# Values with the values held in TensorE, row sums in four column groups, and one listed order for the opening

## Chip, core and metric

The kernel runs on one NeuronCore of a Trainium2 chip. The metric is the device time of one execution in microseconds. Before the change the median of four runs is 1032.1 us (1031.84 to 1032.41). Smaller is better.

A core has five engines that run at once, each through its own instruction list in order: TensorE (PE, matrix products, with weight loads shown apart as PEld), VectorE (DVE), ScalarE (ACT), GpSimd (POOL) and SyncE (SP, which only issues transfers). They meet at semaphores. TensorE writes its results into eight banks of accumulator memory, and VectorE or ScalarE must copy a result out before the bank can be used again.

## What is computed

Attention of 49,152 query rows (four images of 12,288) over keys that are a pooled and projected image, followed by a gated feed-forward layer:

```python
def _attn_ref(q, kv, w_sr):                      # q (4, 12288, 128), kv (4, 384, 32, 128)
    r = 4
    kv_pool = kv.reshape(B, H // r, r, W // r, r, C).mean(axis=(2, 4))
    kv_flat = kv_pool.reshape(B, -1, C) @ w_sr   # 768 keys for each image
    k = v = kv_flat
    s = (q @ k.transpose(0, 2, 1)) / np.sqrt(C)
    s = s - s.max(-1, keepdims=True)
    a = np.exp(s)
    a /= a.sum(-1, keepdims=True) + 1e-09
    return a @ v

def _moe_ref(x, w_gate, w_val, w_out):           # d_model 128, d_ff 1536
    gate = np.maximum(x @ w_gate, 0.0)
    val = x @ w_val
    return gate * val @ w_out
```

Keys and values are the same 768 x 128 matrix. The feed-forward layer has one property that the change uses: if a row of x is multiplied by a positive number c, gate and val are multiplied by c each, and the output row by c squared.

## The kernel before, in words

**Tiles.** The queries are cut into 96 tiles of 512 rows (T), 24 for each image; four tiles are a group (GRP). The 768 keys are six chunks of 128 (NJC), the 1536 hidden units twelve blocks of 128 (NFB). For a tile k the work is:

- `scores(k, jc)` (line 245): one 512-wide matmul for a chunk of keys, and ScalarE takes the exponential into `aT[k]` (keys by queries, fp16).
- `values(k, jc, half)` (line 252): the exponentials are the weights held in TensorE, the values with one more column of constants stream past, 129 columns, one matmul for each 128 queries and chunk, so 24 in a tile. The extra column gives the row sums. `keep_sums` and `keep_values` (lines 266 and 270) take the reciprocal and multiply, which gives normalised rows `x16`; these are then turned by a DMA transpose (`x_turn`) or, for tiles 0 and 1, on TensorE (`x_turn_pe`, line 287).
- `value_proj(k, fb)` and `gate_proj(k, fb)` (lines 296 and 305): one 512-wide matmul each for a hidden block; ScalarE copies val out, VectorE forms max(gate, 0) x val into `hT`.
- `out_proj(k, fb)` (line 324): twelve matmuls accumulate the output; `out_turn` (line 337) transposes it on VectorE, and POOL multiplies it by the constant 1 / X_SCALE**2 (line 343) before it is stored.

**The loop.** From k = 3 on (LAG) the loop at line 573 goes through twelve steps for each k. In a step it puts out, in this order, one output matmul of tile k - 4, one value matmul of tile k - 3, a score matmul of tile k or values of tile k - 1, and one gate matmul of tile k - 3. The order in the program is the order on every engine (`manual_schedule`, line 412): nothing is rearranged.

**The opening.** Before the loop, lines 415 to 570 handle the first image's keys and tiles 0 to 3 in an order written out by hand. Loads are issued on SP (lines 422 to 429): the key image comes as three pairs of chunks, four pixel lines for each pair; then the first queries. VectorE adds some of the lines and pixels, and TensorE adds up the rest while it transposes them: `turn_add` (line 177) accumulates several transposes into one bank. The result is projected to keys (`project_chunk`, line 198) and turned again to give the values (`turn_values`, line 214). The first four query tiles are cast to fp16 and transposed on TensorE (lines 124 to 139). Tiles 4 and 5 are loaded on SP (`q_load_tile`), cast on POOL and transposed by DMA (`q_cast_turn_tile`, line 114, transposes issued at line 120). The feed-forward weights are loaded on POOL's queue in halves (lines 522 to 525), each half followed by one of those casts; then come the output weights and the rest of group 1's queries (lines 526 to 532). A small copy called `gate` (line 521) holds POOL until the last key lines arrive, so that the weights don't take bandwidth from them.

In the old kernel the opening ends with tiles 0 and 1 finished up to x. The loop's first pass, k = 3, does tile 0's hidden layer together with what is left of the scores and values of tiles 1 to 3 (lines 604 to 615).

Of the kernel before, what the change touches and what calls it, by code (L numbers as in the profile page):

```python
# [16 lines left out]
def kernel(  # L17
# [40 lines left out]
    X_SCALE = 512.0  # L58
    qk_scale = 1.0 / math.sqrt(C)

    assert C == 128 and N % T == 0 and J == 128 * NJC and D_FF == 128 * NFB
    assert NFB == 2 * NJC and NST % GRP == 0 and W // r == 8 and HC == 64

# [9 lines left out]
    q16s, qTs, q32s = {}, {}, {}  # L73
# [25 lines left out]
    def q_load_plain(i0, i1):  # L99
        q32 = work.tile([128, i1 - i0, NS, C], FP32, tag=f"q32_{i0}", bufs=1, name="q32")  # L100
        nc.sync.dma_start(
            q32, q[0, i0 * T : i1 * T, :].rearrange("(p i s) c -> p i s c", i=i1 - i0, s=NS)
        )
        for i in range(i0, i1):
            q32s[i] = q32[:, i - i0]

    def q_load_tile(i):
        q32 = work.tile([128, T], FP32, tag="o_t", bufs=2, name="q32_tile")
        nc.sync.dma_start(
            q32, q[0, i * T : (i + 1) * T, :].rearrange("(t j s) c -> j t (s c)", j=4, s=NS)  # L110
        )
        q32s[i] = q32.rearrange("p (s c) -> p s c", s=NS)

    def q_cast_turn_tile(i):
        g, at = i // GRP, slice(i % GRP * NS, (i % GRP + 1) * NS)
        if g not in q16s:
            q16s[g] = work.tile([128, GRP * NS, C], FP16, tag="q16", bufs=2, name="q16")
            qTs[g] = work.tile([128, GRP * NS, 128], FP16, tag="qT", bufs=3, name="qT")
        nc.gpsimd.tensor_copy(q16s[g][:, at], q32s.pop(i))
        nc.sync.dma_start_transpose(  # L120
            qTs[g][:, at], q16s[g][:, at].rearrange("p s c -> p (s c)")
        )

    def q_cast(i, engine=nc.vector):
        q16 = work.tile([128, NS, C], FP16, tag="q16s", bufs=3, name="q16s")
        if engine is nc.scalar:
            nc.scalar.copy(q16, q32s[i])
        else:
            nc.vector.tensor_copy(q16, q32s[i])
        q16s[0, i] = q16  # L130

    def q_turn_pe(i):
        q16 = q16s.pop((0, i))
        qt_ps = bank([128, NS, 128], FP16)
        for s in range(NS):
            nc.tensor.transpose(qt_ps[:, s, :], q16[:, s, :], ident16)  # L136
        if i == 0:
            qTs[0] = work.tile([128, GRP * NS, 128], FP16, tag="qT", bufs=3, name="qT")
        nc.vector.tensor_copy(qTs[0][:, i * NS : (i + 1) * NS, :], qt_ps)  # L139
# [10 lines left out]
    def kv_load(b, pair, queues=(nc.sync,)):  # L150
        parts = work.tile([128, r, 2, r, C], FP32, tag="kv_in", bufs=3)
# [3 lines left out]
        for dh in range(r):  # L155
            queues[dh % len(queues)].dma_start(  # L156
                parts[:, dh].rearrange("p h dw c -> p (h dw c)"), rows[dh]
            )
        kv_in[b, pair] = parts
# [3 lines left out]
    def pool_pixels(eng, b, pair, h):  # L163
        parts = kv_in[b, pair]
        s2 = work.tile([128, 2, r, C], FP32, tag="kv_s2", bufs=2)
# [11 lines left out]
    def turn_add(chunk, lines, first=False):  # L177

        if first:
# [7 lines left out]
    def turn_end(chunk, lines, engine=nc.vector):  # L187
        turn_add(chunk, lines)
        if chunk % 2 == 0:
            kv_Ts["pair"] = work.tile([128, 2, 128], FP32, tag="kvT", bufs=2, name="kvT")  # L190
        kvT = kv_Ts["pair"][:, chunk % 2]
        if engine is nc.scalar:
            nc.scalar.copy(kvT, kv_Ts[chunk])
        else:
            nc.vector.tensor_copy(kvT, kv_Ts[chunk])
        kv_Ts[chunk] = kvT

    def project_chunk(jc, engine=nc.vector):
        pr = bank([128, 128])
        nc.tensor.matmul(pr, w_sr_f32, kv_Ts.pop(jc), start=True, stop=True)  # L200
        if engine is nc.scalar:
            nc.scalar.mul(kv16[:, 0, jc, 0:C], pr, 1.0 / (r * r))
        else:
            nc.vector.tensor_scalar(kv16[:, 0, jc, 0:C], pr, 1.0 / (r * r), None, op0=ALU.mult)
# [8 lines left out]

    def turn_values(b, pair):
        vt = bank([128, 2, 128], FP16)
        for h in range(2):
            nc.tensor.transpose(vt[:, h], kv16[:, b, 2 * pair + h, 0:C], ident16)
        nc.vector.tensor_copy(kv16[:, b, 2 * pair : 2 * pair + 2, C : 2 * C], vt)
# [26 lines left out]
    def scores(k, jc):  # L245
        if jc == 0:
            aTs[k] = work.tile([128, NJC, T], FP16, tag="aT", bufs=4, name="aT")
# [39 lines left out]
    def x_turn_pe(k):  # L287
        x16 = x16s.pop(k)
        xt_ps = bank([128, NS, 128], FP16)
        for s in range(NS):  # L290
            nc.tensor.transpose(xt_ps[:, s, :], x16[:, s, :], ident16)  # L291
        xT = work.tile([128, NS, 128], FP16, tag="xT", bufs=5, name="xT")
        nc.vector.tensor_copy(xT, xt_ps)
        xTs[k] = xT.rearrange("c s p -> c (s p)")
# [10 lines left out]
    def gate_proj(k, fb):  # L305
        if fb == 0:
# [8 lines left out]
        if fb == NFB - 1:  # L315
            xTs.pop(k)
# [20 lines left out]
    def out_turn(k):  # L337
# [5 lines left out]
        nc.gpsimd.tensor_scalar(  # L343
            o_sb.rearrange("t j s c -> t s j c"),
            o_t.rearrange("t (s j c) -> t s j c", s=NS, j=4),
            1.0 / X_SCALE**2, None, op0=ALU.mult,
        )
# [70 lines left out]
    nc.gpsimd.tensor_copy(ident16, ident)  # L418
    nc.gpsimd.memset(kv16[:, :, :, 2 * C : 2 * C + 16], 1.0 / X_SCALE)

    w_sr_f32 = const.tile([128, C], FP32)
    kv_load(0, 0, (nc.sync, nc.scalar))
    nc.sync.dma_start(w_sr_f32, w_sr)
    for i in range(0, GRP, 2):
        q_load_plain(i, i + 2)
    for pair in range(1, NJC // 2):
        kv_load(0, pair)
    for i in range(GRP, GRP + 2):
        q_load_tile(i)
# [20 lines left out]
    def attend(k, pair):  # L450
        for jc in (2 * pair, 2 * pair + 1):
            for half in range(2):
                values(k, jc, half)

    def line(pair, dh, h=slice(0, 2)):
        return kv_in[0, pair][:, dh, h]

    def add_lines(pair):
        s2 = work.tile([128, 2, r, C], FP32, tag="kv_s2", bufs=2, name="kv_s2")
        nc.vector.tensor_tensor(s2, line(pair, 0), line(pair, 1), op=ALU.add)  # L460
        return s2

    def add_pixels(s2, halves=(slice(0, 2),)):
        s1 = work.tile([128, r, C], FP32, tag="kv_s1", bufs=2, name="kv_s1")
        s1 = s1.rearrange("p (h i) c -> p h i c", h=2)
        for h in halves:
            nc.vector.tensor_tensor(s1[:, h], s2[:, h, 0:2], s2[:, h, 2:4], op=ALU.add)
        return s1

    def scores_of(k, pair):  # L470
        for jc in (2 * pair, 2 * pair + 1):
            scores(k, jc)

    s1 = add_pixels(add_lines(0))
    for h in range(2):
        turn_add(h, line(0, 2, h), first=True)
    for h in range(2):
        turn_add(h, s1[:, h])
    for h in range(2):
        turn_end(h, line(0, 3, h), (nc.vector, nc.scalar)[h])  # L480
    for h in range(2):
        project_chunk(h, (nc.vector, nc.scalar)[h])
    for i in range(2):
        q_cast(i, (nc.vector, nc.scalar)[i])
        q_turn_pe(i)
    scores_of(0, 0)
    scores_of(1, 0)
    for i in range(2, GRP):
        q_cast(i)
    q_turn_pe(2)  # L490
    turn_values(0, 0)
    q_turn_pe(3)
    scores_of(2, 0)
    scores_of(3, 0)

    halves = (slice(0, 1), slice(1, 2))

    def add_third(pair, s2, h):
        nc.vector.tensor_tensor(s2[:, h], s2[:, h], line(pair, 2)[:, h], op=ALU.add)  # L499

    s2 = add_lines(1)
    for h in halves:
        add_third(1, s2, h)
    s1 = add_pixels(s2, halves)
    attend(0, 0)
    for h in range(2):
        turn_add(2 + h, line(1, 3, h), first=True)
    for h in range(2):
        turn_end(2 + h, s1[:, h], nc.scalar)
    for h in range(2):  # L510
        project_chunk(2 + h, nc.scalar)
    s2 = add_lines(2)
    for k in range(GRP - 1):
        scores_of(k, 1)
    add_third(2, s2, halves[0])
    s1 = add_pixels(s2, halves)
    turn_values(0, 1)
    turn_add(5, line(2, 2, 1), first=True)

    gate = const.tile([128, 1], FP32)  # L520
    nc.gpsimd.tensor_copy(gate, line(2, 2)[:, 0, 0, 0:1])
    for own in (slice(0, D_FF // 2), slice(D_FF // 2, D_FF)):
        nc.gpsimd.dma_start(wv16[:, own], moe_w_val[:, own])
        nc.gpsimd.dma_start(wg16[:, own], moe_w_gate[:, own])
        q_cast_turn_tile(GRP + (own.start > 0))
    nc.gpsimd.dma_start(wo16, moe_w_out.rearrange("(fb f) c -> f fb c", f=128))
    rows = q[0, GRP * T : 2 * GRP * T, :].rearrange("(i t j s) c -> j t i s c", i=GRP, t=32, s=NS)
    for j in range(4):
        nc.gpsimd.dma_start(
# [153 lines left out]
```

The softmax here doesn't subtract the row's maximum and nothing guards it: scores larger than these inputs give would overflow.

## Time and profile before

| | us |
|---|---|
| median of four runs | 1032.1 (1031.84 to 1032.41) |
| the profiled execution, its time | 1031.84 |
| its span in the profile | 1030.1 |
| first matmul of the key pooling (line 182) | 8.95 |
| first output matmul of tile 0 (line 333) | 37.60 |
| VectorE busy in the span | 912.9 (89%) |
| ScalarE busy in the span | 908.9 (88%) |

The profile shows one execution, instruction by instruction. Its times count from the start of the span; the time of a run is a little longer than the span, since it also has what lies around it. "Busy" of TensorE counts a matmul from its start to the modelled end of its result, and consecutive matmuls overlap: a 512-wide one takes 379 ns from start to end, but the next starts after about 216. So for a chain of matmuls the distance between starts is the price of one, not its duration. The granted clock is 1.00 in all stretches that are used here.

Three ways of looking at it are used below. A table by stretches gives the busy time of every engine between two moments. The chain that ended last goes back from the last instruction, at each step to what released it. The groups of instructions by line give their number, mean duration and the idle time ahead of them.

### The profile page before, as it was taken

To read this page: it belongs to the slowest core of one execution; us is meant where nothing else is said; L and a number is where in the kernel's file an instruction comes from. 1 tells how busy PE (TensorE), PEld (TensorE's weight loads), DVE (VectorE), ACT (ScalarE), POOL (GpSimd) and SP (SyncE) were. 2 spreads that over 40 slices of the span, in tenths; PEclk is the share of its full clock that TensorE was granted. 3 is DMA by queue.
4 is the path that set the end of the run, shared out by engine and by line. 5 is a ranking of instruction groups with operands and counts; after the bars stand their busy time and mean duration, and the time that the engine had idled before them with its cause. 6 is when DMAs were issued, how large, how long until landed. Compare 5 with 4: busy or idle time off the path is not lost.

```text
span 1030.1 us, 20013 instructions
## 1 busy us (share of the span) xinstructions
PE 1021.8 (99%) x6560; PEld 543.7 (53%) x6560; DVE 912.9 (89%) x1676; ACT 908.9 (88%) x1745; POOL 280.5 (27%) x289
## 2 busy tenths in 40 slices
PE   8999999999999999999999999999999999999998
PEld 5555555555555555555555555555555555555555
DVE  4889898998989898998989898999898898989898
ACT  4988988888898888888888889888888988889887
POOL 1412146521211124642212121664121221111110
PEclk9999999999999999999999999999999999999999
DMA  8936386462542558726345266683653533513222
GB/s 316 121 59 81 93 189 142 77 93 41 86 73 44 78 121 161 169 52 91 55 65 86 34 85 141 143 170 57 86 71 48 73 53 67 87 33 64 34 42 53
DMA packets 328896, 93.60 MB, mean 91 GB/s; under 512 B 308568, under 2 KB 321752, under 8 KB 328792
## 3 DMA queue, kind: packets, MB, share of 16 engines
q1 hardware_dynamic: 313672, 78.24, 39.3%
q0 software_dynamic: 14688, 12.98, 10.8%
q8 instruction: 51, 0.84, 0.3%
q10 hardware_dynamic: 432, 1.11, 0.3%
q14 instruction: 53, 0.43, 0.2%
HBM read 53.94 MB, written 26.35 MB: 78 GB/s over the span
## 4 chain that ended last, share of the span: by engine, by line
PE 98%; DMA 1%; DVE 0%; ACT 0%; issue 0%; SPq 0%; ACTq 0%
PE bank_ps L298 24%; PE bank_ps L309 24%; PE bank_ps L333 23%; PE bank_ps L260 13%; PE bank_ps L249 12%; PE bank_ps L319 1%; DMA parts<-in_kv_dram 1%; PE bank_ps L182 0%; PE bank_ps L208 0%; PE bank_ps L200 0%; DVE kv_s L499 0%; DVE kv_s L460 0%; SPq L156 0%; PE bank_ps L136 0%; PE bank_ps L291 0%
## 5 line engine op out<-in xcount | busy, mean ns | idle before, releaser
L312 DVE SCALAR_TENSOR_TENSOR hT<-bank_ps,val 128x512 f16<-128x512 f32 x1152 | 757.9, 686 | 90.9 <-ACT val L302 70.6
L302 ACT CAST val<-bank_ps 128x512 f16<-128x512 f32 x1152 | 677.5, 589 | 102.5 <-PE bank_ps L298 100.5
L298 PE MATMUL bank_ps<-xT,wv 128*128 128x512 f16 x1152 | 436.6, 379 | 0.1
L309 PE MATMUL bank_ps<-xT,wg 128*128 128x512 f16 x1152 | 436.6, 379 | 0.0
L333 PE MATMUL bank_ps<-hT,wo 128*128 128x512 f16 x1116 | 423.0, 379 | 0.0
L250 ACT ACTIVATE aT<-bank_ps 128x512 f16<-128x512 f32 x576 | 345.8, 604 | 1.5 <-PE bank_ps L249 1.2
L343 POOL TENSOR_SCALAR o_sb<-o_t 128x512 f32<-128x512 f32 x93 | 138.3, 1487 | 693.9 <-DVE rinv L268 658.1
L260 PEld LDWEIGHTS <-aT 128*128 128x128 f16 x2304 | 177.0, 98 | 132.4
L260 PE MATMUL bank_ps<-kv,aT 128*128 128x129 f16 x2304 | 222.8, 220 | 0.0
L249 PE MATMUL bank_ps<-qT,kv 128*128 128x512 f16 x576 | 216.7, 379 | 0.2 <-DVE qT L139 0.2
L298 PEld LDWEIGHTS <-wv 128*128 128x128 f16 x1152 | 112.7, 98 | 132.3
L309 PEld LDWEIGHTS <-wg 128*128 128x128 f16 x1152 | 112.7, 98 | 67.2 <-DVE x L276 0.2
L333 PEld LDWEIGHTS <-wo 128*128 128x128 f16 x1116 | 109.2, 98 | 65.7
L249 PEld LDWEIGHTS <-kv 128*128 128x128 f16 x576 | 56.1, 98 | 67.8 <-issue 0.7
L276 DVE TENSOR_TENSOR x<-bank_ps,rinv 128x256 f16<-128x256 f32 x190 | 80.6, 424 | 6.6
L341 DVE STREAM_TRANSPOSE o_t<-bank_ps 128x512 f32<-128x512 f32 x93 | 65.7, 706 | 0.0
L86 POOL DMA_DIRECT2D q<-in_q_dram x84 | 46.0, 553 | 0.3 <-issue 0.3
L167 POOL TENSOR_TENSOR s<-parts 128x512 f32<-128x512 f32 x36 | 44.8, 1265 | 0.0
L268 DVE RECIPROCAL rinv<-bank_ps 128x2 f32<-128x2 f32 x192 | 28.1, 146 | 1.2 <-PE bank_ps L260 1.2
L169 POOL TENSOR_TENSOR s<-s 128x512 f32<-128x512 f32 x18 | 22.8, 1267 | 1.4
L171 POOL TENSOR_TENSOR c<-s 128x256 f32<-128x256 f32 x18 | 13.1, 725 | 1.4
L319 PEld LDWEIGHTS <-hT 128*128 128x128 f16 x144 | 10.2, 98 | 5.8
(54 smaller groups left out, 96.9 us busy)
## 6 DMA issues: line engine op xcount, KB each, us to landing
parts<-in_kv_dram SPq DMA_DIRECT2D x46, 512.0 KB, 6.8
out_dram<-o_sb SPq DMA_DIRECT2D x353, 64.0 KB, 2.2
q<-in_q_dram POOLq DMA_DIRECT2D x84, 128.0 KB, 4.9
xT<-x SPq DMA_TRANSPOSE x94, 2.5
out_dram<-o_sb SPq DMA_DIRECT2D x80, 16.0 KB, 1.5
placed<-blocks SPq DMA_DIRECT2D x9, 128.0 KB, 1.8
kvT<-placed SPq DMA_DIRECT2D x36, 32.0 KB, 1.9
parts<-in_kv_dram ACTq DMA_DIRECT2D x2, 512.0 KB, 7.2
```

The lines of the kernel that those rows point to most:

```text
L86: nc.gpsimd.dma_start(q16[32 * j : 32 * (j + 1)].rearrange("t (i s) c -> t i s c", i=GRP), rows[j])
L249: nc.tensor.matmul(s_ps, kv16[:, k // NST, jc, 0:C], qT_of(k), start=True, stop=True)
L250: nc.scalar.activation(aTs[k][:, jc, :], s_ps, AF.Exp, scale=qk_scale)
L260: nc.tensor.matmul(x_ps[:, i, :], aTs[k][:, jc, s * 128 : (s + 1) * 128], kv16[:, k // NST, jc, C : 2 * C + 1], start=(jc == 0 and i == 0) ...
L276: nc.vector.tensor_tensor(x16s[k][:, 2 * half : 2 * half + 2, :], x_ps[:, :, 0:C], rinv.to_broadcast([128, 2, C]), op=ALU.mult,)
L298: nc.tensor.matmul(va_ps, wv16[:, fb * 128 : (fb + 1) * 128], xTs[k], start=True, stop=True)
L302: nc.scalar.copy(val, va_ps)
L309: nc.tensor.matmul(g_ps, wg16[:, fb * 128 : (fb + 1) * 128], xTs[k], start=True, stop=True)
L312: nc.vector.scalar_tensor_tensor(hTs[k][:, fb, :], g_ps, 0.0, vals.pop((k, fb)), op0=ALU.max, op1=ALU.mult)
L333: nc.tensor.matmul(o_banks[k], wo16[:, fb, :], hTs[k][:, fb, :], start=fb == 0, stop=fb == NFB - 1)
L341: nc.vector.transpose(o_t, o_banks.pop(k))
L343: nc.gpsimd.tensor_scalar(o_sb.rearrange("t j s c -> t s j c"), o_t.rearrange("t (s j c) -> t s j c", s=NS, j=4), 1.0 / X_SCALE**2, None, ...
```

## The change

It touches only tiles 0 to 3 and the order of the opening. Beyond that, the loop is the same.

1. **Values.** For tiles 0 to 3 the values are held in TensorE and the exponentials stream past, 512 wide: six matmuls for each tile (`lead_values`) in place of 24, and the result comes out turned already, without normalisation. One copy (`lead_kept`) makes it the input of the feed-forward layer.
2. **Row sums.** Since the extra column is gone, the sums come from matmuls with a 128 x 32 block of ones as weights (`lead_sums`), one for each tile and chunk, 24 in all. Tile k uses the 32 columns of the array from 32k on and writes 32 partitions of one shared bank. They come in two pieces: U0 (five chunks, 20 matmuls) and U1 (the last chunk, four).
3. **Scale at the end.** VectorE turns the sums, takes the reciprocal and squares it; POOL spreads it in 16 small copies (`lead_scales`, R in the list). In `out_turn` POOL multiplies the output of these tiles by that scale, broadcast over 32 columns, in place of the constant.
4. **One list.** The whole opening is one list of words. T0.1 is the transposing of line 1 of chunk 0, T2.p that of pixel sums; a, b, c and p are sums on VectorE; kvT, pj, key, vt and val are the steps to keys and values of a chunk; cast, qt and qT those of the queries; S, V, v and g are scores, values, value and gate projection of a tile; W0 and W1 the weight halves, wo the output weights with the rest of the queries. Keys and values now go chunk by chunk. Tile 0's whole hidden layer and three score matmuls of tile 4 (S4.5, S4.0, S4.2) are in the list; the loop starts at k = 4 and leaves out the scores done. Pooling uses other sums: chunks 0, 1 and 3 entirely by transposes on TensorE, chunk 4 partly, chunks 2 and 5 on VectorE.
5. **Loads.** Queries 2 and 3 are loaded ahead of 0 and 1. W1 is issued before the cast of tile 4, and wo with the remaining queries before the cast of tile 5.

```diff
+    LEAD = GRP
+    OPENING = """
+        T0.1 T1.0 T0.0 T0.2 cast2 T1.2 T1.1 T0.3 cast0 kvT0 qt2 T1.3 cast3 cast1 gate22 W0 W1
+        cast4 qT4 wo cast5 qT5 qt3 pj0 qt0 qT2 kvT1 pj1 key0 qT3 key1 qt1 qT1 S2.0 S3.1 qT0 vt1
+        T3.0 vt0 a2 val1 S3.0 val0 T3.1 S1.1 S2.1 b2 V3.1 S0.1 V3.0 c2 T3.2 S1.0 V2.0 T3.3 kvT3
+        p2 S0.0 V1.0 pj3 V2.1 T2.p key3 V1.1 kvT2 vt3 val3 S3.3 pj2 key2 a4 S2.3 V0.0 V0.1 S0.3
+        S0.2 S1.3 p4 a5 V2.3 S3.2 V3.3 b5 T4.2 V0.3 c5 T4.p T4.3 vt2 kvT4 val2 S2.2 S1.2 p5 pj4
+        V3.2 key4 T5.p kvT5 S0.4 V0.2 S3.4 vt4 pj5 val4 V1.3 key5 S1.4 V0.4 vt5 val5 S0.5 S2.4
+        V3.4 S3.5 S2.5 S1.5 V0.5 U0 xT0 v0.5 V3.5 v0.3 xT3 U1 R v0.1 V1.4 v0.2 g0.5 g0.2 v0.0
+        V2.2 S4.5 g0.3 v0.4 V2.4 v0.11 g0.4 v0.7 g0.1 g0.11 v0.8 v0.9 V1.2 v0.6 g0.7 V2.5 g0.0
+        V1.5 xT1 v0.10 g0.9 xT2 g0.10 S4.0 g0.6 S4.2 g0.8
+    """.split()
...
+    def lead_values(k, jc):
+        first = k not in x_banks
+        if first:
+            x_banks[k], x_count[k] = bank([128, T]), 0
+        x_count[k] += 1
+        nc.tensor.matmul(
+            x_banks[k], kv16[:, 0, jc, C : 2 * C], aTs[k][:, jc, :],
+            start=first, stop=x_count[k] == NJC,
+        )
+
+    def lead_kept(name, k):
+        xTs[k] = work.tile([128, NS, 128], FP16, tag="xT", bufs=5, name="xT").rearrange("c s p -> c (s p)")
+        copy_on(name, xTs[k], x_banks.pop(k))
+
+    def lead_sums(chunks):
+        if "sums" not in x_banks:
+            x_banks["sums"] = bank([128, T])
+        for jc in chunks:
+            for k in range(LEAD):
+                nc.tensor.matmul(
+                    x_banks["sums"][32 * k : 32 * (k + 1), :], ones, aTs[k][:, jc, :],
+                    start=jc == 0, stop=jc == NJC - 1, skip_group_check=True,
+                    tile_position=(0, 32 * k),
+                )
+
+    def lead_scales():
+        turned = work.tile([128, NS * 4, 32], FP32, tag="o_sb", bufs=3, name="sums_turned")
+        nc.vector.transpose(turned.rearrange("p x m -> p (x m)"), x_banks.pop("sums"))
+        inverse = const.tile([128, NS * 4], FP32)
+        nc.vector.reciprocal(inverse, turned[:, :, 0])
+        square = const.tile([128, NS * 4], FP32)
+        nc.vector.tensor_tensor(square, inverse, inverse, op=ALU.mult)
+        for k in range(LEAD):
+            for b in range(4):
+                nc.gpsimd.tensor_copy(
+                    lead_scale[32 * b : 32 * (b + 1), k], square[32 * k : 32 * (k + 1)]
+                )
...
+        if k < LEAD:
+            scale = lead_scale[:, k].rearrange("t (s j o) -> t s j o", s=NS, o=1)
+            nc.gpsimd.tensor_tensor(to, o_by, scale.to_broadcast([128, NS, 4, 32]), op=ALU.mult)
+        else:
+            nc.gpsimd.tensor_scalar(to, o_by, 1.0 / X_SCALE**2, None, op0=ALU.mult)
...
-    for k in range(LAG, last + 1):
+    for word in OPENING:
+        open_step(word)
+    nc.gpsimd.tensor_copy(gate, hTs[0][:, NFB - 1, 0:1])
+    q_load(2)
...
+    for k in range(LEAD, last + 1):
...
-            elif step % 2 == 0:
-                if k < NT:
+            if step % 2 == 0:
+                if k < NT and (k, step // 2) not in done:
                     scores(k, step // 2)
```

Each engine takes its instructions from the list in the list's order. Copies and sums go to VectorE unless a table gives them to ScalarE (kvT0, kvT1, kvT2, kvT5, key2, val3, cast3, qT0, qT2, xT1, xT2) or POOL (the casts of tiles 1, 2, 4 and 5). `aT` has five buffers now instead of four.

## The prediction

> **What bounds the kernel now.** I read three things in this order: the busy times, the busy time by stretch, and the chain that ended last.
>
> ```profile
> PE 1021.8 (99%) x6560; PEld 543.7 (53%) x6560; DVE 912.9 (89%) x1676; ACT 908.9 (88%) x1745; POOL 280.5 (27%) x289
> ```
>
> TensorE bounds everything, so only two things can move the time: how much TensorE work there is, and how long TensorE waits. The stretches (columns: stretch, length, busy us and instructions of PE, weight loads, DVE, ACT, POOL, then clock, DMA share, GB/s) show where it waits.
>
> ```profile
> 8.95:13.00 4.05, 3.64 (x28) 2.98 (x28) 0.98 (x4) 1.04 (x3) 0.00 (x0) 1.00 1.02 409
> 13.00:16.00 3.00, 2.75 (x21) 1.47 (x22) 2.62 (x8) 2.18 (x6) 0.00 (x0) 1.00 1.03 410
> 16.00:20.29 4.29, 3.56 (x27) 2.40 (x25) 3.77 (x6) 2.66 (x7) 0.00 (x0) 1.00 1.02 409
> 20.29:24.00 3.71, 3.71 (x27) 2.73 (x28) 2.29 (x6) 3.36 (x8) 1.40 (x3) 1.00 0.78 203
> 24.00:28.00 4.00, 4.00 (x52) 3.14 (x50) 1.12 (x5) 3.37 (x8) 1.61 (x3) 1.00 0.63 119
> 37.60:46.68 9.08, 9.08 (x44) 4.09 (x43) 8.64 (x16) 9.08 (x19) 2.36 (x5) 1.00 0.63 102
> ```
>
> After 20.29 us TensorE has no hole worth a tenth. What can be won lies before that, in the opening; the start of tile 0's output projection (L333, first matmul at 37.60 in the timeline) is the mark against which I measure. The chain names what fills the holes:
>
> ```profile
> 1.49 7.42 DMA parts<-in_kv_dram
> 8.95 2.40 PE bank_ps L182 x20
> ...
> 15.71 1.23 DVE kv_s L460
> 16.93 0.02 issue
> 16.95 1.29 DVE kv_s L499 x2
> 18.25 0.35 DVE kv_s L467
> 18.59 0.04 issue
> 18.64 0.78 PE bank_ps L182 x4
> ```
>
> Until 8.95 it is the first key rows arriving, and from 15.71 to 18.59 it is VectorE, summing pooled lines while TensorE has nothing to do.
>
> **Price list, from starts in the timeline and chain.** A 512-wide fp16 matmul: 42 of them fill 37.60 to 46.68, so 0.216. A 129-wide one: 16 in 0.91 in the chain, 0.057. A 128-wide fp16 transpose: two in 0.11, 0.056. An fp32 transpose of one pixel: four start between 9.87 and 10.31, 0.110. A key projection: two chunks in 0.83, 0.41. Loads lie under the matmuls:
>
> ```profile
> L298 PE MATMUL bank_ps<-xT,wv 128*128 128x512 f16 x1152 | 436.6, 379 | 0.1
> L298 PEld LDWEIGHTS <-wv 128*128 128x128 f16 x1152 | 112.7, 98 | 132.3
> L260 PE MATMUL bank_ps<-kv,aT 128*128 128x129 f16 x2304 | 222.8, 220 | 0.0
> ```
>
> **Before, 8.95 to 37.60 (28.65 us).** Work: 48 fp32 transposes 5.28, 6 projections 2.46, 16 q, 6 value and 8 x transposes 1.68, 24 scores and 24 hidden-layer matmuls 48 x 0.216 = 10.37, 96 value matmuls 5.47. Sum 25.26, so 3.4 us of holes.
>
> **After, part by part.** *Pooling on TensorE.* The listed order has 16 transposes each for chunks 0, 1 and 3, 10 for chunk 4, 2 each for chunks 2 and 5: 62 in place of 48, 1.5 us more. But T0.1, T1.0 and T0.0 (12 of them, 1.3) need only lines 0 and 1, on which VectorE's first sum already started at 6.38; they fall into the hole before 8.95. Leaves 50, 5.50. The VectorE sums of the first pair (1.23 and 0.69) vanish; those of the second pair shrink to 3 sums of 0.69 and one of 0.42 for chunk 2.
> *Values.* 96 x 0.057 = 5.47 become 24 x 0.216 = 5.18; the 8 x transposes (0.45) go, and so do the normalising reciprocals and multiplications of tiles 0 to 3 on VectorE and ScalarE.
> *Row sums (U).* 24 new matmuls of 32 columns. No row shows matmuls in separate column groups. From below: 24 starts at the shortest spacing any row has, 0.056, 1.34 in all. From above: one after another with the load uncovered, 24 x (0.216 + 0.098) = 7.5; with loads covered, as in the L298 rows, 5.18. A gain is excluded: the old sums rode along as column 129. I take 1.34: the four groups of a chunk write disjoint partitions.
> A rule that speaks against it: the Trainium skill, "TensorEngine Tiling (Array Packing)", Key Properties, says that changing the tiling mode drains TensorE, and "TensorE: Matmul & The Clock Gate", Part 3, gives 2.38x for three column tiles and lets a weight load pass under a running matmul only if its row group differs. The L298 rows disagree with the last point, 98 ns loads lying under matmuls in the same rows with 0.1 us idle over 1152. By those pages I estimate 1.7 (1.34 x 3 / 2.38) plus four drains of 0.16, 2.3 in all, which moves the forecast below by nothing.
> *Moved.* Tile 0's whole first layer and three score matmuls of tile 4 (S4.5, S4.0, S4.2) stand before the loop. So 27 scores, 24 hidden, 24 values: 75 x 0.216 = 16.20; 22 small transposes 1.23; projections 2.46. Sum with U: 5.50 + 2.46 + 1.23 + 16.20 + 1.34 = 26.73, of which 0.65 is later saved in the loop (39 matmuls in place of 42): 26.1 net, 0.8 more than before.
> *Holes left.* Laying the listed order out with these durations, each engine in its own order, leaves 0.9 before S4.5: 0.45 for the first q casts (pair 2-3 usable at 10.34 plus POOL's 0.61 cast), 0.1 before the first scores, the rest eight small waits on VectorE and ScalarE copies. The same laying-out of the old order gives 37.4 for the measured 37.60.
>
> **The new wait.** S4.5 needs the transposed queries of tile 4. They come as before: load, POOL cast, DMA transpose issued on SP.
>
> ```profile
> L120 SPq DMA_TRANSPOSE qT<-q x1: 1317/1317/1317, 25.8 to 25.8; - x1
> ...
> DMA to landing us min/median/max: 7.0/7.0/7.0
> ```
>
> Landed at 25.8 + 7.0 = 32.8. The old kernel first used them at 38.05 (L249), so nobody saw it. In the listed order TensorE reaches S4.5 after 50 fp32 transposes, 6 projections, 22 small ones, 24 scores, 20 values, 7 hidden matmuls and U: 5.50 + 2.46 + 1.23 + 51 x 0.216 + 1.34 = 21.55, at 8.95 + 21.55 + 0.9 = 31.4. Everything behind it on TensorE stands: g0.3, v0.4, and with them ScalarE's val copies and VectorE's gate products. On POOL's queue the second weight halves (W1) now go out before cast4, and wo and four query loads before cast5: W1 can be done sooner and wo collides more. Bounds for the landing: 25.8 plus the 4.4 of the second L120 transpose, 30.2; and 35, if wo and the queries add some 2 us. Its own row, 32.8, is the nearest; I take 32.5, as W1 leaves the queue earlier.
> Then 3 scores, 4 values and 17 hidden matmuls, 24 x 0.216 = 5.18, and 0.2 of waits on ScalarE (12 evictions of about 0.48 in 5.2 us): the loop starts at 32.5 + 0.05 + 5.18 + 0.2 = 37.9, worth 37.3 after the 0.65. Against 37.60: 0.3 less. This stall also covers U: up to 1.34 + 1.1 = 2.4 U costs nothing; without the cover each us of it counts.
>
> **Costed at nothing.** Output scaling of tiles 0 to 3 becomes a POOL multiplication by a broadcast: 1.49 (L343) against 1.27 for a POOL sum of that size (L167); even doubled it lies in a tile's 10.42 us. The 16 POOL copies of the scales precede q_load(2), whose tile 8 comes four tiles later. wv's and wg's first halves landed at 27.5 and 29.2 (issued 20.8 and 21.5, 6.7 and 7.7 on the way), before v0.5 (28.7) and g0.5 (30.5) in the laid-out order; their second halves and wo (30.1 + 6.0 = 36.0) are issued 3 to 4 us earlier now, and wo is needed at 37.9; if a weight half is late, TensorE stands for as long. After tile 4 the loop is the same.
>
> **Forecast (A).** The profiled execution took 1031.84 with a span of 1030.1; the median is 1032.1, 0.3 above. Median less 0.3: 1031.8. What the opening gains is given back at S4.5. Own range 1031.1 (landing 31.8) to 1032.7 (landing 33.4).
>
> **Rivals.** *B, slower: the row sums run one after another.* U is 5.18 instead of 1.34: S4.5 is reached at 35.2, no stall, loop at 40.6, worth 40.0, +2.4: 1034.5; with uncovered loads +4.7, 1036.8. It decides from U above 2.4, and passes 0.2% from about 4.8. For: no row shows otherwise. Against: disjoint column groups.
> *C: the transpose lands by 31.4.* No stall: loop at 31.4 + 5.18 + 0.2 = 36.8, worth 36.1, -1.5: 1030.6; with the 0.2 and two thirds of the 0.9 gone too, 1029.8. For: the second L120 took 4.4 only. Against: the tile 4 and 5 loads, weights and transposes share the queues between 22 and 33.
> *D: it lands at 34 to 35.* +1.2 to +2.2, 1033.3 to 1034.3. For: wo and query loads 3 to 4 us earlier than before, in the same stretch. Against: W1 is out of the way sooner.
>
> **Chances.** A 0.42, B 0.26, C 0.22, D 0.10. What a measurement can tell here is about 0.2%, 2.1 us. Faster: 0.13 of C. Slower: 0.21 of B, 0.05 of D, 0.26. Within: 0.61. Range 1030.2 to 1034.8: it leaves out the best of C and the worst of B.
>
> **What would show it.** Starts of the ones matmuls 0.06 apart in fours (A, C, D) or 0.216 (B); a TensorE hole of about 1 us ended by the DMA transpose just before tile 4's first score; no hole over 0.2 between 12 and 31 us; first L407 matmul near 37.9. It is wrong if the weight halves or a PSUM bank hold TensorE earlier, or if ScalarE is late in the tail.

## The result and the profile after

The changed kernel takes 1034.1 us (median of 32 runs, 1032.64 to 1036.68) against 1031.91 for the kernel before (52 runs, 1031.61 to 1033.08): ratio 1.0020, 95% interval 1.0015 to 1.0025. Forecast was 1031.8. So it is 2.2 us slower, where 0.3 us faster was expected. The profiled execution took 1033.97 us, with a span of 1031.7.

The busy times of the page, against those shown of before: TensorE has 42 matmuls fewer and is still busy for 99%.

```profile
PE 1024.0 (99%) x6518; PEld 542.0 (53%) x6518; DVE 908.7 (88%) x1665; ACT 909.6 (88%) x1743; POOL 283.8 (28%) x308
```

The same stretches as before, and two later ones (stretch, length, then busy us and instructions of PE, weight loads, DVE, ACT, POOL; clock, DMA share, GB/s):

```profile
8.95:13.00 4.05, 3.92 (x41) 3.47 (x41) 1.04 (x4) 1.44 (x4) 1.48 (x2) 1.00 1.03 410
13.00:16.00 3.00, 3.00 (x23) 2.01 (x21) 2.08 (x7) 2.68 (x6) 0.00 (x0) 1.00 1.03 411
16.00:20.29 4.29, 4.29 (x27) 2.52 (x26) 2.67 (x7) 3.53 (x9) 0.00 (x0) 1.00 1.04 412
20.29:24.00 3.71, 3.09 (x20) 1.80 (x18) 2.40 (x6) 2.26 (x6) 2.82 (x5) 1.00 0.74 190
24.00:28.00 4.00, 4.00 (x23) 2.10 (x22) 1.49 (x6) 3.79 (x8) 3.17 (x5) 1.00 1.83 208
28.00:32.00 4.00, 4.00 (x36) 1.36 (x34) 2.56 (x6) 3.74 (x8) 1.27 (x4) 1.00 1.56 78
32.00:36.00 4.00, 1.80 (x9) 0.79 (x9) 1.80 (x4) 1.77 (x5) 2.97 (x16) 1.00 1.30 162
```

The holes of before (VectorE's sums, up to 20.29) are gone: 3.00 of 3.00 and 4.29 of 4.29. Two new ones stand in their place, 0.6 us between 20.29 and 24 and 2.2 us between 32 and 36. The waits of TensorE in the opening name both (line, what it waited for: us, times, longest):

```profile
PE bank_ps L294 <- DMA qT<-q: 2.2, 1, 2.2
PE bank_ps L227 <- DMA kv_in<-in_kv_dram: 0.6, 1, 0.6
```

The chain that ended last goes through the first of them (start, us, what):

```profile
12.78 12.00 DMA q_late<-in_q_dram
24.78 0.05 issue
24.83 0.62 POOL q L98
25.46 0.02 issue
25.47 8.87 DMA qT<-q
34.34 0.05 issue
34.39 0.39 PE bank_ps L294
```

In the kernel before it went through VectorE's sums; here it is the load of tile 4's queries, the cast, the DMA transpose (8.87 us) and S4.5 (now line 294). The matmul ahead of S4.5 starts at 31.81, so S4.5 could start at 32.02. It starts at 34.39: 2.37 us lost (the list of waits says 2.2, since it counts from the modelled end of the matmul ahead). The first output matmul (now line 407) stands at 39.61 where line 333 stood at 37.60.

From there to the time: 2.01 later, less the 0.65 of three scores already done, is 1.36. Some 0.2 more goes right behind, where two matmuls wait for ScalarE: its instructions end at 39.83 and 40.82, the matmuls start at 39.88 and 40.87. The chain shows these two distances as longer than the usual 0.22:

```profile
39.99 0.27 PE bank_ps L374
...
40.91 0.34 PE bank_ps L385
```

The span is 1.6 longer. And 0.3 us lies outside the span: time less span is 2.10 on average over 33 executions of the changed kernel and 1.79 over 33 of the kernel before.

### The profile page after: what moved, and what is told of

The parts are those of the page before. It is cut to its first block, busy times and chain, and to the rows that moved or that the text cites. A ratio compares the mean times of both kernels' runs of the same rounds, so it can differ in the third digit from the quotient of the medians.

```text
span 1031.7 us, 19923 instructions
## 1 busy us (share of the span) xinstructions
PE 1024.0 (99%) x6518; PEld 542.0 (53%) x6518; DVE 908.7 (88%) x1665; ACT 909.6 (88%) x1743; POOL 283.8 (28%) x308
## 4 chain that ended last, share of the span: by engine, by line
PE 96%; DMA 3%; SPq 0%; POOL 0%; issue 0%; ACT 0%; ACTq 0%
PE bank_ps L385 24%; PE bank_ps L374 24%; PE bank_ps L407 23%; PE bank_ps L305 12%; PE bank_ps L294 12%; DMA q_late<-in_q_dram 1%; DMA qT<-q 1%; DMA kv_in<-in_kv_dram 1%; PE bank_ps L393 1%; PE bank_ps L259 0%; SPq L184 0%; SPq L129 0%; PE bank_ps L339 0%; SPq L502 0%; POOL q L98 0%
## 5 line engine op out<-in xcount | busy, mean ns | idle before, releaser
L423 POOL TENSOR_SCALAR o_sb<-o_t 128x512 f32<-128x512 f32 x89 | 132.4, 1487 | 664.8 <-DVE rinv L313 635.8
L305 PEld LDWEIGHTS <-aT 128*128 128x128 f16 x2208 | 170.6, 98 | 130.3
L305 PE MATMUL bank_ps<-kv,aT 128*128 128x129 f16 x2208 | 215.3, 220 | 0.0
L321 DVE TENSOR_TENSOR x<-bank_ps,rinv 128x256 f16<-128x256 f32 x184 | 78.1, 425 | 6.5
L194 POOL TENSOR_TENSOR s<-kv_in 128x512 f32<-128x512 f32 x36 | 44.8, 1264 | 0.0
L421 POOL TENSOR_TENSOR o_sb<-o_t,lead_scale 128x512 f32<-128x512 f32 x4 | 4.2, 1047 | 34.4 <-DVE rinv L313 25.5
```

The source lines that it names most:

```text
L305: nc.tensor.matmul(x_ps[:, i, :], aTs[k][:, jc, s * 128 : (s + 1) * 128], kv16[:, k // NST, jc, C : 2 * C + 1], start=(jc == 0 and i == 0) ...
L321: nc.vector.tensor_tensor(x16s[k][:, 2 * half : 2 * half + 2, :], x_ps[:, :, 0:C], rinv.to_broadcast([128, 2, C]), op=ALU.mult,)
L423: nc.gpsimd.tensor_scalar(to, o_by, 1.0 / X_SCALE**2, None, op0=ALU.mult)
```

## The experiments

Two questions: is the transpose's landing the whole loss, and what made it late? Each run was paired with the kernel before on the same chip.

### The changed kernel again

No edit; the control for the later runs.

> The changed kernel as it is, as a control beside the next three. If its loss is the landing of tile 4's transposed queries, its profile shows again one TensorE hole of 1.5 to 3 us at S4.5 ended by that transfer, and the time is 2 us over the kernel before, with a wider spread than that kernel (1.5 us or more) since a transfer sets it. If the loss were in the list itself, the spread would be as narrow as before.

1034.34 us (1033.92 to 1035.76) against 1032.21, ratio 1.0022 (1.0014 to 1.0031). Landing 8.9 us after the issue; TensorE waits 2.1 us there. The result repeats.

### The three scores back in the loop

```diff
-  V2.2 S4.5 g0.3 ...   xT2 g0.10 S4.0 g0.6 S4.2 g0.8
+  V2.2 g0.3 ...   xT2 g0.10 g0.6 g0.8
```

> The three score matmuls of tile 4 are taken out of the list and done in the loop again. Theory 1 (the whole loss is the wait of S4.5 for tile 4's transposed queries): the 2.4 us hole of TensorE goes, 0.65 us of matmuls move into the loop. First output matmul at 39.6 - 2.4 - 0.65 = 36.6 us, against 37.6 before the change: about 1.0 us less than the kernel before, 1030.9, ratio 0.999. Theory 2 (another wait stands behind it: the weight halves or ScalarE's evictions hold TensorE by about as much): a hole of 1 us or more at g0.3 to g0.11, first output matmul at 38 or later, time 1032.5 to 1034.

1031.88 us (1031.07 to 1032.22) against 1032.13, ratio 0.9997 (0.9988 to 1.0006). The waits in its opening have no line for S4.5 any more:

```profile
PE bank_ps L227 <- DMA kv_in<-in_kv_dram: 1.1, 2, 0.8
PE bank_ps L156 <- POOL q L98: 0.2, 1, 0.2
```

So the stall is the loss: 0.25 faster than before instead of the control's 2.1 slower, it takes back some 2.4 us. But 1030.9 was expected, so a gain of about 1 us that should be left over is missing. The same kernel profiled once more, on another chip:

> The run with the three scores of tile 4 in the loop, profiled a second time. If the landing of tile 4's transpose is settled by the program, it lands again 7.8 us after its issue, its 16 parts within 0.8 us; if it is chance, up to 9.1 us. No hole at the first score of tile 4, the first output matmul of tile 0 near 37.3, span near 1029.8.

Landing again 7.8 us after the issue, the 16 parts within 0.9; first output matmul at 37.7, span 1030.9, 1032.97 us. The hole at the last key line (line 227) was 1.2 this time, 0.4 longer, and the first output matmul came 0.4 later. So that hole varies from run to run and goes straight into the time once the stall behind it is gone. The span is 1.1 longer, though: the other 0.7 came later, in the loop (970.6 us from the first output matmul to the last, against 969.9), and was not followed.

### The scores as the last words of the list

```diff
-  V2.2 S4.5 g0.3 ...   xT2 g0.10 S4.0 g0.6 S4.2 g0.8
+  V2.2 g0.3 ...   xT2 g0.10 g0.6 g0.8 S4.5 S4.0 S4.2
```

> The changed kernel with the three score matmuls of tile 4 (S4.5, S4.0, S4.2) as the last words of the list, behind g0.8, and nothing else moved. They stay in the opening, but TensorE reaches S4.5 only near 37.3 us, after any landing seen so far. If only the place of S4.5 ahead of the landing costs time: no hole at the first score of tile 4, the first output matmul of tile 0 near 37.3 + 0.65 = 38.0, and the time of the run with these scores in the loop, 1031.9 on the other chip (ratio 0.9997), here 0.9990 to 1.0006. If having these scores in the opening at all costs (buffers of the exponentials, banks), then it is slower than that run by 0.5 us or more. Side question: the transpose of tile 4 landed 8.8 to 9.1 us after its issue in the four runs that had S4.5 early and 7.8 us in the two that had it in the loop, with the same order of transfers. If TensorE's own standing at S4.5 goes with the late landing, it is 7.8 here; if the program's shape decides otherwise, 8.8 to 9.1.

1032.38 us (1031.8 to 1033.11) against 1031.85, ratio 1.0005 (0.9995 to 1.0014): no stall, span 1029.8 as with the scores in the loop, first output matmul at 37.65, worth 37.0. It is the place of S4.5 that costs. Whether its being in the opening costs a little too is not settled: the time is 0.5 above 1031.85, the run with the scores in the loop was 0.25 below its own, and the two intervals overlap; the profile shows no such cost (37.0 against 37.3). The transpose landed 9.0 us after its issue although nobody waited for it, so TensorE's standing is not what makes it late.

### Which transfer makes the transpose late

The order on POOL's queue was W0 cast4 W1 cast5 wo before, and W0 W1 cast4 wo cast5 after. Three kernels, S4.5 left in the list:

```diff
-  W0 W1 cast4 qT4 wo cast5 qT5
+  W0 cast4 qT4 W1 cast5 qT5 wo        (the old order)
+  W0 W1 cast4 qT4 cast5 qT5 wo        (wo late)
+  W0 cast4 qT4 W1 wo cast5 qT5        (W1 late)
```

> S4.5 stays in the list, but POOL's queue has the old order: first weight halves, cast of tile 4, second halves, cast of tile 5, output weights and remaining queries. If the moved transfers made the transpose late, it lands after 7.0 us as before, near 32.8, the hole at S4.5 is about 0.9 us, first output matmul near 38.1, time about 1032.5, 1.6 us under the changed kernel. If the transpose is late for another reason (run-to-run, or the new load order of the queries), it takes 8.5 to 9 us again and the time stays at 1034.

> Second weight halves early as in the changed kernel, but output weights and remaining queries after the cast of tile 5 as before. If wo's small packets beside the transpose make it late, it lands near 32 to 32.8 and the time falls to about 1032.3. If the early second halves do, it still takes 8.5 to 9 us, time about 1034.

> Second weight halves after the cast of tile 4 as before, but output weights and remaining queries before the cast of tile 5 as in the changed kernel. If wo beside the transpose makes it late, wo now queues behind the halves and collides less than in the changed kernel but more than before: landing 33 to 34, time 1033 to 1033.6. If the early second halves do, landing near 32.8 and about 1032.5.

| order | issue to landing | TensorE waits for it | first output matmul | time (before 1032.13) | ratio |
|---|---|---|---|---|---|
| changed (control) | 8.9 | 2.1 | 39.74 | 1034.34 (before 1032.21) | 1.0022 (1.0014 to 1.0031) |
| W1 late | 7.9 | 0.8 | 38.84 | 1032.89 | 1.0006 (0.9998 to 1.0015) |
| old order | 7.8 | 0.9 | 38.59 | 1032.63 | 1.0004 (0.9995 to 1.0013) |
| wo late | 6.4 | none | 37.36 | 1032.33 | 1.0000 (0.9992 to 1.0009) |

With W1 early and wo late the transpose lands sooner than with the old order (6.4 against 7.8): W1 out of the way does help. With wo early as well it lands 2.5 us later. wo early while W1 is late costs 0.1. So neither step alone does it. The old order does not bring back the 7.0 of the kernel before (7.1 in its second profile), though: 0.8 of the lateness has another cause in the new list, which no run isolates. The issue of wo in the kernel before (timeline):

```profile
30.05 1.04 POOL L526 DMA_DIRECT2D wo<-in_moe_w_out_dram  x1
```

and in the changed one:

```profile
25.39 1.04 POOL L589 DMA_DIRECT2D wo<-in_moe_w_out_dram  x1
```

That is 0.08 ahead of the transpose's own issue at 25.47, and 539 of wo's 1536 packets had started by 32.0 us. With W1 late it was issued 1.0 behind the transpose, with W1 still ahead of it, and 16 had started by then. This fits that wo meets the transpose only once W1 has left the queue; no run isolates it. The differences of about 1 us in the table rest on one profile for each of the last three orders. The times agree with them: of W1 late the slowest run took 1033.46, of the control the fastest 1033.92.

The transfers between 25.5 and 35 us, for the changed kernel (queue: packets, MB, time of its packets as a share of the span of 16 engines; then issues with KB and us to landing):

```profile
q0 software_dynamic: 2166, 1.05, 144.5%
q1 hardware_dynamic: 842, 0.31, 30.9%
...
wo<-in_moe_w_out_dram POOLq DMA_DIRECT2D x1, 384.0 KB, 9.2
...
qT<-q SPq DMA_TRANSPOSE x2, 7.6
```

and with wo late:

```profile
q0 software_dynamic: 1932, 0.89, 72.4%
q1 hardware_dynamic: 1144, 0.37, 34.5%
...
wo<-in_moe_w_out_dram POOLq DMA_DIRECT2D x1, 384.0 KB, 5.8
...
qT<-q SPq DMA_TRANSPOSE x2, 5.5
```

POOL's queue (q0) moved 1.05 MB against 0.89, but its packets took twice as long altogether. The packet records show where. From 29.5 to 31 us of the changed kernel 119 of wo's 256-byte packets had medians of 0.2 to 0.57 us in each half microsecond, against 0.04 to 0.05 from 31 on. The transpose is 512 packets of 256 bytes on q1. Of these 350 had started by 28.5 us, none started in the next microsecond, and the last did at 32.04. With wo late 382 had started by 28.0, none started in the next microsecond either, and the 512th did at 30.96. The 16 parts of the transpose landed between 32.36 and 34.34, and with wo late within 0.1 us of each other. That packets of the two queues are under way at the same time, and that wo's take long and the transpose's start later than with wo late, is seen; how a packet of the one holds up the other was not isolated.

One thing stays open. With the changed order of transfers the landing took 8.8 to 9.1 us in all five profiles with these scores in the list, and 7.8 in all three with them in the loop. No run tells why. With wo late it took 6.4 with them in the list and 6.3 with them in the loop (the kernel with three edits, below), so wo's early issue costs the landing 1.5 to 2.5 us in either place.

### Row sums tile by tile

```diff
-        for jc in chunks:
-            for k in range(LEAD):
+        for k in range(LEAD):
+            for jc in chunks:
```

> The row sums U0 go tile by tile (five chunks of one tile one after another) in place of chunk by chunk, so matmuls that follow each other use the same column group. If the speed of the sums comes from four column groups side by side, they start 0.216 us apart and U0 takes 4.3 us in place of 1.1. TensorE then reaches S4.5 at about 35.2, after the transpose has landed (34.3): the hole goes, and the time rises by 0.9 us over the changed kernel only (0.4 to 1.7), because the hole covers the rest. If nothing is covered, it rises by 3.2 us. If column groups don't matter, starts stay 0.004 us apart.

1033.8 us (1033.32 to 1034.89) against 1032.21, ratio 1.0016 (1.0007 to 1.0025). The timeline of the changed kernel at U0 (start, us, what):

```profile
28.22 1.26 PE L353 MATMUL bank_ps<-aT,ones 128*32 128x512 f16 x20
29.42 0.39 PE L374 MATMUL bank_ps<-xT,wv 128*128 128x512 f16 x1
```

and of this kernel:

```profile
29.43 1.95 PE L353 MATMUL bank_ps<-aT,ones 128*32 128x512 f16 x20
31.31 0.39 PE L374 MATMUL bank_ps<-xT,wv 128*128 128x512 f16 x1
```

From the first row sum to the next line it is 1.20 us in the one and 1.88 in the other: 0.7 more, not the 3.2 of a serial order. The recorded starts come in eight rounds some 0.22 us apart, of 1, 2, 3, 4, 4, 3, 2 and 1 matmuls, where the other order has five rounds of four. That fits each group starting its five one round after the group before; three rounds more are 0.65. The trace doesn't name the group of a start. The longer sums cost no time here: TensorE arrived later at S4.5 and waited 0.4 there instead of 2.1 (its hole at the key line was longer too, 1.35 us against 0.76). To see its price without that cover, the same edit with the three scores in the loop:

> The same order of the sums, with tile 4's scores in the loop, so that no hole covers it. Compared with the kernel that has only the scores moved (1031.9 on its chip, 0.25 us under the kernel before), the whole price shows: 3.2 us more, 1035, about 2.9 us over the kernel before. Rival: the list waits for ScalarE or the weights at that place anyway and takes back part of it, 1 to 2 us more.

1032.68 us against 1032.21, ratio 1.0003 (0.9994 to 1.0012); against the run with the scores in the loop alone some 0.6 us more, within what two such ratios can tell from none. Serial row sums, rival B, are out in both orders.

### The second hole: twenty more instructions

The last four transposes of chunk 4 (T4.3) wait for the last key line. The timeline of the changed kernel:

```profile
22.94 0.66 PE L227 MATMUL bank_ps<-ident,kv_in 128*128 128x128 f32 x4 [0.62 <-DMA kv_in<-in_kv_dram]
```

By the landings of its parts, 15 of the 16 engines had brought that line by 21.69, one came at 22.90; before, all were there at 21.86. The transfers between 20 and 21.5 us hold one packet of the instruction queue (q8) in the changed kernel:

```profile
q1 hardware_dynamic: 133, 0.42, 72.7%
q8 instruction: 1, 0.02, 4.5%
```

and none in the kernel before:

```profile
q1 hardware_dynamic: 146, 0.46, 77.4%
```

That packet is 16 KB, started at 20.28 and took 1.09 us. Before, the first such packet came at 24.95, when all key lines had landed. There are 51 of this size in the execution, for 13,036 matmuls and weight loads, one in about 256, so more instructions on TensorE ahead of it should pull it forward. Twenty 128x128 matmuls on the identity were added behind the warm-up matmuls (nothing reads them):

```diff
+    for _ in range(20):
+        nc.tensor.matmul(idle[:, 0:128], ident16, ident16, start=True, stop=True)
```

> Twenty small matmuls (40 instructions with their loads, 1.1 us) are put behind the warm-up into an unused bank. In the profiles so far the 16 KB fetch of the instruction queue at 20.3 to 20.5 us falls on the transfer of the last key lines, and one of 16 DMA engines lands them 1.2 to 1.6 us after the others; in the kernel before it falls at 24.9 and the last line lands in 0.8 us on all. If the fetch makes that engine late and comes at a fixed place in TensorE's instruction list, it now comes earlier, near 17.5 to 19 us, and an earlier line (pair 2, line 0 to 2) is the first with one late engine. If the late engine has another cause (the weight transfers, say), the fetch moves but line 3 stays the first that is late.

One execution: 1033.94 us beside 1031.86. The packet moved to 18.07, and the first key line with a straggling engine is now two lines earlier: 15 engines had brought it by 19.22, the last came at 20.40 (all by 19.16 in the changed kernel). The two lines behind it straggle as well: 15 engines had brought them by 20.47 and 21.72, the last came at 21.65 and 22.89. The wait at T4.3 has gone from the list of waits:

```profile
PE bank_ps L294 <- DMA qT<-q: 2.0, 1, 2.0
PE bank_ps L156 <- ACT q L96: 0.2, 1, 0.2
```

That isn't because its line came sooner (22.89 against 22.90): TensorE reached this part of the list 1.0 us later (T4.2 at 22.31 against 21.29), so that the lateness no longer showed. What the edit shows is that the straggling began at an earlier line when the packet came earlier. So the instruction packet delays key lines, as far as one profile and the two kernels above tell; the records don't say on which engine the packet ran. The time didn't move, since S4.5 still waited for the landing.

### Both holes taken out

Scores in the loop, wo late, and T4.3 moved behind other work:

```diff
-  W0 W1 cast4 qT4 wo cast5 qT5 ...   V0.3 c5 T4.p T4.3 vt2 kvT4 val2 S2.2 S1.2 p5 pj4 V3.2 key4 T5.p
+  W0 W1 cast4 qT4 cast5 qT5 wo ...   V0.3 T4.p vt2 val2 c5 S2.2 S1.2 V1.3 T4.3 kvT4 V3.2 p5 pj4 key4 V0.2 T5.p
```

> Three edits together: tile 4's scores in the loop, output weights after the cast of tile 5, and the last key line of chunk 4 (T4.3) read about 0.65 us later in the list, after vt2, S2.2, S1.2 and V1.3, with the sum c5 behind val2. In the profiles so far TensorE stands 0.7 to 1.1 us at T4.3, because that line lands on one DMA engine 1.2 us after the others. If that hole is the rest of the loss, it shrinks to 0.2 or less and the time falls by 0.7 us to 1.0 us under the kernel before (1031.1). If ScalarE's exponentials are next behind it, only 0.2 us comes out of it (1031.6 to 1031.8), with small waits on ScalarE after 24 us.

1032.06 us (1031.17 to 1033.17) against 1032.21, ratio 0.9999 (0.9990 to 1.0007); first output matmul at 36.75, the earliest of all, span 1029.3. T4.3 no longer waits long, but VectorE's copy is late next, one matmul on (timeline):

```profile
23.12 0.66 PE L227 MATMUL bank_ps<-ident,kv_in 128*128 128x128 f32 x4
23.61 0.38 PE L339 MATMUL bank_ps<-aT,kv 128*128 128x512 f16 x1
24.23 0.49 PE L241 MATMUL bank_ps<-kvT_chunk,w_sr_f 128*128 128x128 f32 x2 [0.24 <-DVE kvT_chunk L98]
```

The distances ahead of this one and of the score at 26.18 give back about 0.6 us. In the span this kernel is 0.8 ahead of the kernel before, in the time of its profiled execution (1031.55) 0.3 ahead of 1031.84, and in the median 0.15. Some 0.35 to 0.5 of the gain goes outside the span.

### Time outside the span

> The kernel before, unchanged, profiled a second time. Its profiled execution had a span of 1030.06 us and a time of 1031.84, 1.78 outside the span; the changed kernel and its variants had 1.9 to 2.25 outside. If that is a property of the programs, this run again shows about 1.8; if it scatters from run to run, up to 2.2.

1031.93 us with a span of 1030.2: 1.73. Over all runs the kernel before has 1.79 outside the span on average (1.73 to 1.85), and the changed kernel and its variants 2.07 to 2.19 (1.85 to 2.32). It is a property of the programs, worth 0.3 us. The trace holds the span alone, so the cause isn't shown.

## Why the prediction failed, step by step

**The step that failed** is the size of one term: "Its own row, 32.8, is the nearest; I take 32.5, as W1 leaves the queue earlier." The landing was at 34.34, 1.84 later. Of the 1.9 by which the transpose took longer than its old 7.0, 1.1 goes with the moved transfers (wo early 2.5 more, W1 early 1.4 less), and 0.8 stays with the old order too and is open. The place and kind of the new wait were right, and the chain of the changed kernel shows them as forecast. The sign that W1 was given was right too (6.4 against 7.8 with wo late). But the text had already said that "wo collides more" and then priced that at nothing. It also put wo's issue 3 to 4 us earlier than before; it came 4.7 earlier (25.39 against 30.05), beside the transpose's own. Rival D, which priced it, gave 1033.3 to 1034.3; measured 1034.1. With the measured landing in the prediction's own sum, 0.3 less becomes 1.5 more; 0.3 outside the span, which no step had, makes 1.8, and the waits on ScalarE behind the first output matmuls 2.0, against 2.1 between the two profiled executions. That 1034.1 lies inside the wide range (1030.2 to 1034.8) is in good part luck: its upper end went with rival B (1034.5), which didn't come, and D, which did, had a chance of 0.10.

**Work.** The pooling holes vanished as forecast, and from S4.5 to the first output matmul it took 5.22 us (5.38 forecast with its waits). S4.5 was reached at 32.0, not 31.4: the "holes left" knew nothing of the key line's late engine (0.6), and the row sums took 0.4 more. About 0.4 of what it had counted ahead of S4.5 did not come. The old kernel's trace couldn't show the late engine, since its instruction packet came after the keys.

**Row sums.** 1.34 was taken. Measured are 1.20 and 0.33 for the two pieces, and 0.09 ahead of each: 1.7. The starts are 0.003 to 0.004 apart in fours and 0.216 from four to four, so the column groups do run side by side; the 0.4 above 1.3 is at the four changes, about 0.1 each. The Trainium skill ("TensorEngine Tiling (Array Packing)", Key Properties: changing the tiling mode drains TensorE) agrees with that in so far as time is lost at each of the four changes; that a drain is the cause isn't shown. The prediction's estimate of 0.16 for each is high, and so is its 2.3 in all. The difference, 0.4, was covered by the stall, as the prediction said of U up to 2.4.

**Rival C** did not come about, but the runs without a stall test its price (1030.6), which was too good. Without a stall the runs gave 1031.9 (scores in the loop), 1032.3 (wo late) and 1032.4 (scores last). The first is 1.3 above 1030.6. Without the stall's cover three costs come through that the price left out: 0.8 at the key line, 0.4 of the row sums' mode changes and 0.3 outside the span. They add up to 1.5, a little more than what is missing.

**Costed at nothing.** The broadcast multiplication on POOL took 1.05 us, less than the 1.49 of the constant one (groups by line; the mean in ns follows the busy us):

```profile
L423 POOL TENSOR_SCALAR o_sb<-o_t 128x512 f32<-128x512 f32 x89 | 132.4, 1487 | 664.8 <-DVE rinv L313 635.8 <-DMA qT<-q 15.8 <-DMA out_dram<-o_sb 13.2
...
L421 POOL TENSOR_TENSOR o_sb<-o_t,lead_scale 128x512 f32<-128x512 f32 x4 | 4.2, 1047 | 34.4 <-DVE rinv L313 25.5 <-DVE o_t L415 8.9
```

TensorE waited for no weight half and no wo. These were right, but wo's earlier issue had a cost elsewhere: it fell on the transpose that stands ahead of S4.5.

## What to carry to other kernels

Once the first use of a transfer is pulled forward to its landing time, the landing is no longer free: price each transfer that the same change moves into its path, not only its own row, and price them together. Here, against the old order's 7.8 us, one move alone took 1.4 off the landing, the other alone put 0.1 on, and both together put on 1.1. And when TensorE's work is packed closer, look at what was just in time by luck: a load that needs all 16 engines is as late as its latest engine.

## What the runs showed of the hardware

- Matmuls of four column groups run side by side even when the program lists five in a row for one group: 20 of them took 1.88 us in that order and 1.20 in the interleaved one, against 4.32 for 20 at 0.216.
- An instruction packet of 16 KB took about 1.1 us. While all 16 engines are loading, the line it meets comes about that much later on one of them (22.90 against 21.69 for the last of the others), and with the packet moved to 18.07 so did the two lines after (21.65 against 20.47, 22.89 against 21.72).
- DMA transposes of one and the same shape (128x512) landed 4.4 to 9.1 us after their issue. With one load moved behind the next cast the same transpose took 6.4 in place of 8.9.
